# One core, linear attention beside a gated GLU: the last down products of two token groups in seven instead of eight, with their operands formed earlier

## The chip, the cores and the metric

The kernel runs on one core of a Trainium2 chip. The metric is the device time of one execution in microseconds (us), as the median of several runs. Five engines of the core work side by side: TensorE does the matrix products (PE; the load of the operand that stands in the array is shown apart as PEld), VectorE does sums (DVE), ScalarE copies, rounds and evaluates functions (ACT), GpSimd (POOL) and SyncE (SP) issue transfers here. Each engine takes its instructions in the order written.

## The reference

For x of 2048 tokens by 640:

```
g   = sigmoid(sum(x * gate_w))                       # one number a token
q, k, v = x @ wqkv, in 32 heads of 20
phi(t) = where(t > 0, t + 1, exp(t)) + 1e-6
a   = (phi(q) @ (phi(k)^T @ v)) / (phi(q) @ sum(phi(k)) + 1e-6)  @ wo
b   = (sigmoid(x @ w_gate) * (x @ w_up)) @ w_down    # 640 -> 1536 -> 640
out = g * a + (1 - g) * b
```

## The kernel before

**Products.** All operands of the large products are held as a high and a low part in fp32r, and one product of a 128x128 block with 512 tokens is three matmuls: high by high, high by low, low by high (helper `mm3`, lines 406 to 408). The high part of an operand is an ACT copy that rounds (line 419), the low part a DVE subtraction (line 423); the helper `split` does both.

**Fewer products by Strassen's scheme.** Two by two blocks of a product are computed in seven products of sums in place of eight. The names S1 to S4 are sums of blocks of the weight, T1 to T4 sums of blocks of the other operand, A11, B22 and so on are blocks. A partial sum that two results share is computed once, and a result that needs it as its start gets it by an ACT copy from one PSUM bank to another (`seed`); the PE then adds the next product on top of it.

**Stages.** First the k stage (to about 180 us) forms k, v and the weights of the MLP; four chunks of x pass through it, and each chunk's Strassen forms are made in it. Weights whose forms are used twice go to DRAM as formed parts and come back later. Then the 2048 tokens are taken in two halves of two groups of 512: groups 2 and 3 (`pr` is 1 in the code) from about 180 to 405 us, groups 0 and 1 (`pr` is 0) from about 405 us to the end. For each half there is a q phase (q, its feature map) and an f phase that goes through 12 blocks f of 128 of the 1536 hidden columns: gate and up products, sigmoid and product give the hidden block hf; after every second block a pair of f blocks goes down (`down_pair`): its contribution to the 5 x 2 output blocks (5 blocks of 128 output columns, 2 token groups) is added to tb in SBUF by DVE.

**The last pair.** In the pairs before the last, four of the five output blocks are computed in seven products for each two by two set (14 products) and the fifth plainly (4 products), 18 in all. For groups 0 and 1 this holds for the last pair too; its S forms are made during their f phase (`queue_last_s`: two loads, four DVE sums, two splits, two stores to DRAM, then two loads). Three of its outputs are not added by DVE but by a POOL transfer that accumulates into tb (`far`). For groups 2 and 3 the last pair is plain: `last_down` issues 2 x 5 x 2 = 20 products, and in its course queues the scaling of tb by 1 - g (omg, `scaled`) and its store to b_dram.

**Order.** The class `Order` keeps a model of the clock of each engine. Work for ACT and DVE is queued with a cost and a key; `order.fill` places queued work where the model sees room beside the products, `order.need` places it at once because what follows wants it, `order.run` places one item of a kind. Transfers are put on the SP or POOL queue at the place where the code issues them, and a transfer that has to wait holds up those behind it on its queue. Tiles come from pools with a fixed number of buffers, so a load waits for the last reader of the tile that it overwrites.

**Names.** hf: hidden operand or a T form; wd: formed down weights, ds: formed S sums; dst, wst_f: raw weights; rot, dd, cc, ch: PSUM banks (two each); cx, c: intermediate sums; xth and xtl: T forms of x (high, low), fac and wst: raw x in the q phase.

## Time and profile before

| | before |
|---|---|
| median of 3 runs | 728.75 us (728.59 to 729.23) |
| the profiled execution | 728.59 us; its span is 726.9 us, and 1.7 us lie around it |
| PE | 722.2 us busy, 99% of the span, 3563 matmuls |
| DVE | 573.0 us, 79%, 1006 instructions |
| ACT | 364.0 us, 50%, 675 |
| POOL | 101.2 us, 14%, 166 |
| DMA | 176.95 MB, mean 243 GB/s |

How to read the rows: an instruction of the timeline has its start, its duration, engine, line, operation, output<-inputs and shape; what stands in square brackets is the idle time of the engine before it and what ended it. A group of instructions has its count, busy time and mean ns. Matmuls are pipelined: each is shown with 0.39 us, but the next starts 0.227 us after it, and the step from start to start is what counts.

### The profile page before, as it was taken

Reading aid. Unit: us, or ns where it says so; the run is one execution under the profiler, and the core shown is the slowest. Engines: PE = TensorE matmul, PEld = TensorE weight load, DVE = VectorE, ACT = ScalarE, POOL = GpSimd, SP = SyncE. Lnnn points to the kernel's source line nnn. Section 1 sums busy time; section 2 is a strip of 40 time slices with the busy share of each in tenths; the row PEclk is TensorE's granted clock in tenths of the full one; section 3 lists DMA queues with packets and bytes.
Section 4 is the critical chain, followed back from the end, with each engine's and each line's share of the span. In section 5 each row is a group of like instructions: output and inputs, shape, how many; then the busy total and the mean of one; then the engine's idle time right before and its main releaser. Section 6 shows DMA issues by size and latency. Waiting matters only on the chain.

```text
span 726.9 us, 10146 instructions
## 1 busy us (share of the span) xinstructions
PE 722.2 (99%) x3563; PEld 620.8 (85%) x3563; DVE 573.0 (79%) x1006; ACT 364.0 (50%) x675; POOL 101.2 (14%) x166
## 2 busy tenths in 40 slices
PE   9999999999999999999999999999999999999997
PEld 8999999988888888888888888888888888888886
DVE  6889778987687889898989973447585968698895
ACT  6884649357656653535355363454333232354451
POOL 0211101113212211211210031001000001212000
PEclk9999999999999999999999999999999999999999
DMA  8665658698787866567687289879799695979612
GB/s 258 160 181 111 184 130 252 151 338 295 268 313 259 332 223 232 194 223 253 255 322 273 94 295 331 312 233 311 238 329 358 213 363 169 309 280 291 245 59 102
DMA packets 74137, 176.95 MB, mean 243 GB/s; under 512 B 11834, under 2 KB 35402, under 8 KB 70502
## 3 DMA queue, kind: packets, MB, share of 16 engines
q1 hardware_dynamic: 56102, 111.56, 47.7%
q0 software_dynamic: 17840, 64.57, 25.3%
q8 instruction: 28, 0.46, 0.3%
q14 instruction: 23, 0.19, 0.1%
q10 hardware_dynamic: 144, 0.16, 0.1%
HBM read 105.53 MB, written 64.97 MB: 235 GB/s over the span
## 4 chain that ended last, share of the span: by engine, by line
PE 99%; DVE 0%; issue 0%
PE ch L406 11%; PE ch L407 11%; PE ch L408 11%; PE cc L406 9%; PE cc L407 9%; PE cc L408 9%; PE dd L406 7%; PE dd L408 7%; PE dd L407 7%; PE rot L406 6%; PE rot L407 6%; PE rot L408 6%; PE rot L1505 1%; PE rot L494 0%; PE ch L2576 0%; PE cc L2576 0%
## 5 line engine op out<-in xcount | busy, mean ns | idle before, releaser
L419 ACT ACTIVATE c<-ch 128x512 f32<-128x512 f32 x52 | 31.1, 598 | 90.6 <-PE ch L408 90.5
L423 DVE TENSOR_TENSOR hf<-c,hf 128x512 fp32r<-128x512 f32 x78 | 53.1, 687 | 21.5 <-ACT hf L419 21.2
L419 ACT ACTIVATE hf<-c 128x512 fp32r<-128x512 f32 x78 | 47.7, 625 | 26.0 <-DVE c L423 26.0
L423 DVE TENSOR_TENSOR c<-cc,c 128x512 f32<-128x512 f32 x40 | 27.6, 689 | 34.5 <-PE cc L408 22.3
L406 PE MATMUL ch<-xth,ws 128*128 128x512 f32 x112 | 43.7, 390 | 0.0
L408 PE MATMUL ch<-xth,ws 128*128 128x512 f32 x112 | 43.6, 389 | 0.0
L407 PE MATMUL ch<-xtl,ws 128*128 128x512 f32 x112 | 43.6, 389 | 0.0
L423 DVE TENSOR_TENSOR tb<-rot,tb 128x512 f32<-128x512 f32 (+1 forms) x61 | 39.1, 675 | 3.0 <-PE rot L408 3.0
L423 DVE TENSOR_TENSOR c<-c,c 128x512 f32<-128x512 f32 x50 | 34.4, 688 | 3.3 <-ACT c L419 2.7
L406 PE MATMUL dd<-xrh,wg 128*128 128x512 f32 x90 | 35.2, 391 | 0.0
L408 PE MATMUL dd<-xrh,wg 128*128 128x512 f32 x90 | 35.0, 389 | 0.0
L407 PE MATMUL dd<-xrl,wg 128*128 128x512 f32 x90 | 35.0, 389 | 0.0
L419 ACT ACTIVATE c<-dd 128x512 f32<-128x512 f32 x22 | 13.2, 598 | 41.1 <-PE dd L408 41.1
L423 DVE TENSOR_TENSOR tb<-dd,tb 128x512 f32<-128x512 f32 x40 | 27.4, 686 | 7.7 <-PE dd L408 7.6
L406 PE MATMUL cc<-xbh,ws 128*128 128x512 f32 x84 | 32.7, 389 | 0.0
L408 PE MATMUL cc<-xbh,ws 128*128 128x512 f32 x84 | 32.7, 389 | 0.0
L407 PE MATMUL cc<-xbl,ws 128*128 128x512 f32 x84 | 32.7, 389 | 0.0
L419 ACT ACTIVATE dd<-ch 128x512 f32<-128x512 f32 x22 | 12.8, 582 | 33.6 <-PE ch L408 33.6
L423 DVE TENSOR_TENSOR wst<-wst 128x256 f32<-128x256 f32 (+2 forms) x69 | 27.4, 413 | 1.4
L408 PEld LDWEIGHTS ch<-xth,ws 128*128 128x128 f32 x112 | 21.0, 188 | 4.7
L407 PEld LDWEIGHTS ch<-xtl,ws 128*128 128x128 f32 x112 | 21.0, 188 | 4.2
L406 PEld LDWEIGHTS ch<-xth,ws 128*128 128x128 f32 x112 | 21.0, 188 | 4.1
(663 smaller groups left out, 2362.1 us busy)
## 6 DMA issues: line engine op xcount, KB each, us to landing
wf<-ws POOLq DMA_DIRECT2D x12, 1152.0 KB, 7.6
ws<-wf SPq DMA_DIRECT2D x11, 1152.0 KB, 8.6
wst<-wst_f SPq DMA_DIRECT2D x12, 640.0 KB, 5.1
wf<-wg POOLq DMA_DIRECT2D x12, 640.0 KB, 6.9
wd<-wd POOLq DMA_DIRECT2D x12, 640.0 KB, 8.0
wg<-wf SPq DMA_DIRECT2D x12, 640.0 KB, 5.7
wf<-wd SPq DMA_DIRECT2D x10, 640.0 KB, 9.2
xnst<-xn SPq DMA_DIRECT2D x16, 320.0 KB, 4.2
```

The lines of the kernel that those rows point to most:

```text
L406: nc.tensor.matmul(out, l_hi, r_hi, start=first, stop=False, skip_group_check=True)
L407: nc.tensor.matmul(out, l_hi, r_lo, start=False, stop=False, skip_group_check=True)
L408: nc.tensor.matmul(out, l_lo, r_hi, start=False, stop=last, skip_group_check=True)
L419: nc.scalar.activation(out, src, fn, **kw)
L423: nc.vector.tensor_tensor(out, a, b, op=op)
L1505: nc.tensor.matmul(ps[:w, :w], v[:, m, :w], gt[:, m, c0:c0 + w], start=(m == 0), stop=(m == KC - 1))
```

## The change

Four parts:

1. **The last pair of groups 2 and 3** is computed in 18 products like that of groups 0 and 1 (`last_pair` for both, `last_down` and `tail_f` are gone). The order of its products is its own: W, X0, X1, V, Y0, Y1, W, Z0, Z1, W, X0, X1, Z0, Z1, R0, R1, U0, U1, where V is seeded from W, Y from X, R from X, U from R. V, Y0 and Y1 go out by `far`.
2. **Its S forms** are made in the k stage (`queue_ls`), once for both halves: two loads, four DVE sums and four splits of 256 columns, four POOL stores. `queue_last_s` is gone from the f phase of groups 0 and 1. For groups 2 and 3 `load_last_s` loads them (two of 512 KB) on SP, where the last reader of the tile ds allows it.
3. **The T forms of x's second chunk**, which the q phase of groups 0 and 1 needs, are stored to DRAM in the k stage (`store_t`, eight stores on SP) and loaded again (`load_t`, eight loads on SP behind the S forms), in place of four sums and four splits of 512 columns.
4. **What moves with it**: the scaling of tb is queued in the q phase (`queue_scaled`, step 7), its factor is loaded on the POOL queue instead of SP's; the stores of the last two formed wd tiles come behind the pair (`last_stores`); the steps that turn the attention's denominators into a factor (`queue_dens`) are taken at once when they are ready, instead of in their chain's turn, and the loads of that factor come ahead of down weights (wf) on SP.

The heart of the diff:

```diff
+        def store_t(self, *ts):
+            for t in ts:
+                for i, f in enumerate(self.f.t_part(t, self.cs)):
+                    sp.dma_start(xt_dram[:, t, i], f32(f))
...
+    def queue_ls():
+        p, w = FC // 2 - 1, 4 * P
+        wd_dram[p] = dram.tile([P, 2, WF], F32, name=f"wd{p}")
+        raw = qs.tile([P, 2, D], F32, name="qraw", tag="qraw")[:, :, :w]
+        for j in range(2):
+            sp.dma_start(raw[:, j], wst_f[2 * p + j, :, 2, :w])
...
+            split(t[:, 0], t[:, 1], raw[:, j, 2 * q * P:2 * (q + 1) * P])
+            order.then(lambda: gp.dma_start(wd_dram[p][:, :, 2 * D + cs.start:2 * D + cs.stop], f32(t)))
...
-            if c > 1 and n in (2, 5,):
+            for _ in range(({1: 1, 2: 1, 3: 1, 5: 1}, {3: 2, 4: 1, 5: 1})[c - 2].get(n, 0) if c > 1 else 0):
                 order.run("qw")
...
-            pass
+            chunks[1].store_t(1, 0)
...
+                chunks[1].store_t(2, 3)
                 chunks[2].queue()
...
+            if c == 2 and u == 9:
+                queue_ls()
...
-                          lambda g=g, n=n: st["at", g, KC + n](), chain=True)
+                          lambda g=g, n=n: st.get(("at", g, KC + n), lambda: 1e9)(), **{"first" if n else "chain": True})
...
+    def load_last_s(pr=1):
+        p = FC // 2 - 1
+        if pr:
+            t = down_pool[1].tile([P, 2, 8 * P], F32R, name="ds", tag="ds")
+            DS[p] = [t[:, c] for c in range(2)]
+        else:
+            DS[p] = [x2_tile("ds", F32R).rearrange("p a b -> p (a b)") for _ in range(2)]
+        for c in range(2):
+            sp.dma_start(f32(DS[p][c]), wd_dram[p][:, c, 2 * D:])
...
-    def queue_last_s():
...
+    def load_t(t):
+        c = other[1]
+        for i, f in enumerate(c.f.t_part(t, c.cs)):
+            sp.dma_start(f32(f), xt_dram[:, t, i])
...
         if p == FC // 2 - 1:
+            tags = ("cc", "ch") if pr else ("ch", "ch")
             new("W", "dd", "w0", "B11")
-            new("X0", "ch", "A11", "B11")
+            new("X0", tags[0], "A11", "B11")
             seed("V", "dd", "W")
+            yield
             new("X1", "ch", "A11", "B11", 1)
             seed("Y0", "rot", "X0")
             seed("Y1", "rot", "X1")
             yield
...
+            for q in range(2):
+                go(f"X{q}", "S2", "T2", q=q)
+                if pr:
+                    seed(f"R{q}", "rot", f"X{q}")
+                out(f"X{q}", 2 * q, 1)
...
+            for q in range(2):
+                x = f"R{q}" if pr else f"X{q}"
+                go(x, "S3", "T3", q=q)
+                seed(f"U{q}", tags[q] if pr else "rot", x)
+                out(x, 2 * q + 1, 1)
...
             go("U0", "A22", "T4")
             out("U0", 1, 0)
             go("U1", "A22", "T4", q=1)
             out("U1", 3, 0)
...
-    def last_down(pr, units):
...
-        for i in units:
-            g, o = divmod(i, KC)
-            down_unit(pr, FC - 2, o, g, early.pop(i, None))
...
+    def queue_scaled():
...
+            gp.dma_start(omg[:, g], gate_dram[1, (2 + g) * TG:(3 + g) * TG].partition_broadcast(P))
```

**PE, last pair of groups 2 and 3.** Before, the products of the plain pair alternate over four PSUM banks (dd and rot):

```order
L406 MATMUL rot_4098<-hf,wd 128x512
L407 MATMUL rot_4098<-hf,wd 128x512
L408 MATMUL rot_4098<-hf,wd 128x512
L406 MATMUL dd_4102<-hf,wd 128x512
L407 MATMUL dd_4102<-hf,wd 128x512
L408 MATMUL dd_4102<-hf,wd 128x512
L406 MATMUL rot_4106<-hf,wd 128x512 [waits DVE_49]
```

Now the same place holds the seeded products: X1, V (dd_4125) and Y0 (rot_4133), of which the last two wait for an ACT copy:

```order
L407 MATMUL ch_4129<-hf,wd 128x512
L408 MATMUL ch_4129<-hf,wd 128x512
L409 MATMUL ch_4129<-hf,wd 128x512
L407 MATMUL dd_4125<-hf,wd 128x512 [waits Activation_49]
L408 MATMUL dd_4125<-hf,wd 128x512 [waits DVE_49]
L409 MATMUL dd_4125<-hf,wd 128x512
L407 MATMUL rot_4133<-hf,wd 128x512 [waits Activation_49]
```

And at the end of the pair R0 (rot_4195), R1 (rot_4201) and U0 (cc_4215) follow one another:

```order
L407 MATMUL rot_4195<-hf,ds 128x512 [waits Activation_49]
L408 MATMUL rot_4195<-hf,ds 128x512 [waits DVE_49]
L409 MATMUL rot_4195<-hf,ds 128x512
L407 MATMUL rot_4201<-hf,ds 128x512 [waits Activation_49]
L408 MATMUL rot_4201<-hf,ds 128x512
L409 MATMUL rot_4201<-hf,ds 128x512
L407 MATMUL cc_4215<-hf,wd 128x512 [waits Activation_49]
```

What moved: PE now takes results that it has itself just finished, by way of a copy on ACT, for seven of the 18 products.

**ACT, the same pair.** Before, the sigmoid of the last hidden block (cx<-cx) is the second instruction in the stretch of the pair, and forms for the next phase follow:

```order
L419 ACTIVATE hf<-c_3877 128x512
L419 ACTIVATE cx<-cx 128x512
L419 ACTIVATE hf<-cx 128x512
L419 ACTIVATE xrh<-wst 128x256
L419 ACTIVATE wg<-dst 128x640
```

Now the seeds of V (dd), Y0 and Y1 (rot) stand around that sigmoid, the one of V ahead of it, those of Y behind it:

```order
L420 ACTIVATE hf<-c_3910 128x512
L420 ACTIVATE xah<-wst 128x2x256
L420 ACTIVATE dd_4125<-dd_4117 128x512
L420 ACTIVATE cx<-cx 128x512
L420 ACTIVATE rot_4133<-cc_4121 128x512
L420 ACTIVATE rot_4135<-ch_4129 128x512
L420 ACTIVATE hf<-cx 128x512
L420 ACTIVATE hf<-c_3798 128x512
```

What moved: the copies of which PE has need share ACT's order with the sigmoid, which itself waits for DVE.

**SP, from the last raw weights to the q phase.** Before, the raw weights of q follow those of the last f blocks:

```order
L363 DMA dst<-wst_f 128x640 x2
L363 DMA dst<-wst_q 128x640
L363 DMA wu<-wq_1857 128x768
L363 DMA ws<-wq_1985 128x2304
L363 DMA ds<-gate_dram 128x512 x2
L363 DMA wg<-wq_1854 128x1280
```

Now the S forms and the T forms stand between them, and the factor from gate_dram is gone from this queue:

```order
L364 DMA dst<-wst_f 128x640 x2
L364 DMA ds<-wd_1295 128x1024 x2
L364 DMA xth<-xt_dram 128x2x256
L364 DMA xtl<-xt_dram 128x2x256
L364 DMA xth<-xt_dram 128x2x256
L364 DMA xtl<-xt_dram 128x2x256
L364 DMA xth<-xt_dram 128x2x256
L364 DMA xtl<-xt_dram 128x2x256
L364 DMA xth<-xt_dram 128x2x256
L364 DMA xtl<-xt_dram 128x2x256
L364 DMA dst<-wst_q 128x640
L364 DMA wu<-wq_1890 128x768
```

What moved: ten loads now stand ahead of the weights of the q phase.

More of the change, by code (lines that the diff above doesn't have):

```diff
@@ L1560, in rest @@
         def rest():
-            if j == 0:
+            if p not in wd_dram:
                 wd_dram[p] = dram.tile([P, 2, WF], F32, name=f"wd{p}")
             gp.dma_start(wd_dram[p][:, :, (1 - j) * D:(2 - j) * D], f32(t))
-            if p == FC // 2 - 1:
-                load_d()
-        order.then(rest)
+        if p == FC // 2 - 1:
+            last_stores.append(rest)
+        else:
+            order.then(rest)
     def queue_ds(p):
@@ L1906, in far @@
         def far(key, o, g):
-            if not far_at:
+            if not far_at and order_pr[0]:
+                t = f32(wd_tile())
+                far_at.extend((t[:, 0], t[:, 1], down_pool[1].tile([P, D], F32, name="far", tag="dst", bufs=2)))
+            elif not far_at:
                 far_at.extend(down_pool[1].tile([P, D], F32, name="far", tag=n) for n in ("mr", "mv"))
@@ L1934, in down_pair, with zs @@
             yield
[L1935 to L1938 removed]
+            def zs():
+                new("Z0", "ch" if pr else "cc", "S1", "T1")
+                out("Z0", 1, 1)
+                new("Z1", "cc", "S1", "T1", 1)
+                out("Z1", 3, 1)
+            if not pr:
+                zs()
             go("V", "w1", "B21")
@@ L1966, in down_pair @@
             return
-        if pr:
-            for j in range(2):
-                order.need(("d", ("f", 1, 2 * p + j)))
         new("W", "dd", "w0", "B11")
@@ L2254, in scaled @@
             gp.dma_start(b_dram[:, o, g], tb[:, o, g])
-        for i in units[:4]:
-            g, o = divmod(i, KC)
-            early[i] = ps_tile("rot" if (o + g) % 2 else "dd")
-            down_term(early[i], pr, FC - 2, o, g, True)
-        for i in units:
-            g, o = divmod(i, KC)
-            down_unit(pr, FC - 2, o, g, early.pop(i, None))
+        for i in range(2 * KC):
             order.add(0, v_cost(TG), lambda i=i: scaled(i), ("tb", i),
-                      lambda: order.vec + 0.6, lazy=True)
-            order.fill()
-        order.slack(False)
+                      lambda: max(order.vec + 0.6, order.when(omg)), lazy=True)
     order.need((nx[1], 2))
```

209 lines of the change are left out of this document (95 added, 114 removed).

## The prediction

> **What bounds the kernel now.** I read the page first, then the waits, the timeline of PE at the place of the change, then ACT, DVE and SP there.
>
> ```profile
> PE 722.2 (99%) x3563; PEld 620.8 (85%) x3563; DVE 573.0 (79%) x1006; ACT 364.0 (50%) x675; POOL 101.2 (14%) x166
> PE 99%; DVE 0%; issue 0%
> PE rot L494 <- PEq L2765: 0.8, 1, 0.8
> ```
>
> PE is busy in 99% of the span, the chain that ended last is PE alone, and the one wait of PE lies at the start. So the time is the number of matmuls times their step, and nothing else counts unless it makes PE wait. Work taken from DVE, ACT or a queue is worth nothing here; work added to them costs only where a product then comes late. The profiled execution took 728.59 us, 0.16 under the median of 728.75; the sum below is a difference, and I put it on the median.
>
> The last pair of groups 2 and 3 on PE, first and last product of 20 (60 matmuls), with the last matmul ahead that reads ds, and the first of the q phase:
>
> ```profile
> 389.76 0.39 PE L408 MATMUL cc<-hf,ds 128*128 128x512 f32 x1
> ...
> 392.03 0.39 PE L406 MATMUL dd<-hf,wd 128*128 128x512 f32 x1
> ...
> 405.40 0.39 PE L408 MATMUL rot<-hf,wd 128*128 128x512 f32 x1
> 405.63 0.39 PE L406 MATMUL ch<-xah,wg 128*128 128x512 f32 x1
> ```
>
> From 392.03 to 405.63 are 13.60 us for 60 matmuls: a step of 0.2267 us with no gap, 0.68 us a product.
>
> **The gain.** 18 products in place of 20 are 6 matmuls fewer: 6 x 0.2267 = -1.36 us (0.19%). Nothing else takes matmuls away, so this is also the most that can be won. The Trainium skill, page "TensorE: Matmul & The Clock Gate", section "Back-to-back issue gap", gives 512/2.4 + 2.5, some 216 ns, for an isolated stream of this width; the six would then be worth -1.29 us, an estimate from that page. The rows differ and go first.
>
> **What the new order makes PE wait for.** Plain products start from weights and hidden operands alone. Seven of the new ones start from an ACT copy of a result just finished. The price of such a handover shows at the end of groups 0 and 1, where the same scheme runs already: X0's last matmul, X1, W (dd), then U0, which starts from a copy of X0.
>
> ```profile
> 654.50 0.39 PE L408 MATMUL ch<-hf,ds 128*128 128x512 f32 x1
> ...
> 655.41 0.39 PE L406 MATMUL dd<-hf,wg 128*128 128x512 f32 x1
> ...
> 656.09 0.39 PE L406 MATMUL rot<-hf,wg 128*128 128x512 f32 x1
> 654.99 1.26 ACT L419 ACTIVATE rot<-ch 128x512 f32<-128x512 f32 x2 [2.50 <-PE ch L408]
> L419 ACT ACTIVATE dd<-ch 128x512 f32<-128x512 f32 x22 | 12.8, 582 | 33.6 <-PE ch L408 33.6
> ```
>
> ACT starts 0.49 us after the start of the last matmul that it waits for, and a copy takes 0.58. What follows until PE runs is seen where PE was released by ACT at the last moment:
>
> ```profile
> 178.77 0.60 ACT L419 ACTIVATE c<-ch 128x512 f32<-128x512 f32 x1 [0.19 <-PE ch L408]
> 179.46 0.46 PE L406 MATMUL ch<-xth,wu 128*128 128x512 f32 x1
> 179.75 0.40 PE L407 MATMUL ch<-xtl,wu 128*128 128x512 f32 x1
> ```
>
> The copy ends at 179.37; the matmul stands at 179.46, but the next follows 0.29 after it in place of 0.23, so it ran some 0.06 late: 0.15 from copy to product. A handover is 0.49 + 0.58 + 0.15 = 1.22 us, against 0.2267 for each matmul that stands between.
>
> *U0.* Between R0's last matmul and U0 stands only R1: 4 steps, 0.91 us, where groups 0 and 1 have W as well, 7 steps, 1.59 us and no wait. PE waits 1.22 - 0.91 = 0.31. U1 comes after its own 4 steps plus that 0.31: 0.
>
> *Y0.* X1 and V lie between X0 and Y0 (7 steps), but ACT is not free:
>
> ```profile
> 393.03 0.69 DVE L423 TENSOR_TENSOR cx<-cc,cx 128x512 f32<-128x512 f32 x1
> 393.76 0.63 ACT L419 ACTIVATE cx<-cx 128x512 f32<-128x512 f32 x1 [3.72 <-DVE cx L423]
> 398.76 0.62 ACT L419 ACTIVATE b12h<-wst 128x512 fp32r<-128x512 f32 x1
> 407.25 0.60 ACT L419 ACTIVATE c<-ch 128x512 f32<-128x512 f32 x1 [7.87 <-PE ch L408]
> ```
>
> (b12h there is the last work of ACT before an idle of 7.87 us, so later seeds find it free.) The sigmoid waits for DVE until 393.72, and the seed of Y0 stands behind it. Sigmoids and copies follow each other some 0.1 before the end shown, so the seed runs 394.28 to 394.86 and Y0 can start at 395.01. It is due 12 matmuls after 392.03, at 394.75: a wait of 0.26. Behind it everything on PE moves; the seed of Y1 ends by 395.42 and Y1 is due at 395.69: 0.
>
> *V, Z, R.* V's copy starts at 392.48 + 0.49 = 392.97 and is done at 393.55, V due at 394.07. X0 needs DVE's last read of its bank, tb<-cc:
>
> ```profile
> 391.83 0.69 DVE L423 TENSOR_TENSOR tb<-cc,tb 128x512 f32<-128x512 f32 x1
> 395.87 0.69 DVE L423 TENSOR_TENSOR hf<-cx,hf 128x512 fp32r<-128x512 f32 x1 [0.76 <-ACT hf L419]
> ```
>
> It ends at 392.52 and X0 is due at 392.71: 0, by 0.19. The hidden operand that is formed last (low part done at 396.56; now its high part stands behind both seeds on ACT, so about 396.7) is wanted by the tenth product, 27 matmuls after 392.03 plus 0.26, at 398.4. R0 has 10 steps or more after X0's second product: 0. DVE has fewer additions than before, since three outputs go out by an ACT copy and a POOL accumulate. The accumulates wait for ACT and for DVE's earlier addition; behind them on POOL stand the two stores of formed wd tiles, which are read again only in the f phase of groups 0 and 1, and the q phase's stores.
>
> Sum of the pair: -1.36 + 0.31 + 0.26 = -0.79 us. Bounds of the waits: none at all (if the 0.15 is not paid and DVE is a little earlier), or twice 0.57.
>
> **The load of the S forms.** The two ds loads of 512 KB go out when the last matmul on the old ds ends, 389.76 + 0.39, about 390.2, and Z0, 21 matmuls after 392.03 plus 0.26, wants the first at 397.05, the second at 397.5. Behind them on SP wait eight loads of 256 KB and then the weights of the q phase.
>
> ```profile
> 388.00:391.00 3.00, 3.00 (x15) 2.50 (x14) 3.00 (x6) 2.04 (x4) 0.12 (x1) 1.00 0.00 0
> 394.00:397.00 3.00, 3.00 (x15) 2.47 (x14) 2.14 (x4) 2.18 (x5) 0.00 (x0) 1.00 1.03 411
> 630.86 1.13 SPq L363 DMA_DIRECT2D ds<-wd  x2
> ds<-wd SPq DMA_DIRECT2D x2, 512.0 KB, 7.6
> DMA to landing us min/median/max: 4.6/7.4/10.1
> 390.62 0.33 SPq L363 DMA_DIRECT2D dst<-wst_q  x1
> 396.05 0.72 ACT L419 ACTIVATE wg<-dst 128x640 fp32r<-128x640 f32 x1
> ```
>
> (The first two rows are windows: busy times of PE, PEld, DVE, ACT and POOL, granted clock, DMA share and GB/s; the fifth is of the tile ds.) At 388 to 391 the DMA engines are idle, and 3 us later they move 411 GB/s. Early bound: issue to 391.3 as at 630.86, then 1 MB at 411 GB/s, 2.6 us: 394. Late bound: 10.1 us after the second issue at 391, 401, a wait of 3.6. In between, the median of 7.6, from a stretch with full queues: 398.6, a wait of 1.1. I take 394 to 396, as the row with 0 GB/s is of this very place, and 0. What stands behind is later too: dst<-wst_q went out at 390.62 and was formed from 396.05 on; behind 3 MB at 411 GB/s it lands near 400. Its first reader on PE comes 104 matmuls after 392.03, at 415: covered by 10 us or more.
>
> On this the Trainium skill, page "DMA: Bandwidth & Descriptors", section "Issuing engines are not separate DMA queues", speaks against the change: all transfers run on the same 16 engines and interleave. Its section "Bandwidth" has 6.15 us for 1 MB, by which the loads would land at about 397, an estimate, just in time. Whether the xt loads push in between is the third rival.
>
> **The rest, which I cost at 0 or a risk.** *k stage:* added are 8 + 2 transfers on SP, 4 on POOL, and 4 sums and 4 splits of 256 columns, by the row below 8 x 0.41 = 3.3 us of DVE; moved are qw forms.
>
> ```profile
> L423 DVE TENSOR_TENSOR wst<-wst 128x256 f32<-128x256 f32 (+2 forms) x69 | 27.4, 413 | 1.4
> 60.00:76.00 16.00, 16.00 (x110) 16.00 (x109) 12.00 (x23) 7.47 (x17) 1.19 (x1) 1.00 0.57 138
> 116.00:145.00 29.00, 29.00 (x192) 28.38 (x192) 27.11 (x51) 15.38 (x27) 3.57 (x3) 1.00 0.81 213
> ```
>
> At 60 to 76 DVE has 4 us free in 16 and DMA stands at 0.57, which hides it. At 116 to 145 DVE has 1.9 free in 29: one form late there would stall PE by up to its own 0.7. *q phase:* removed are, among others, these (of 405 to 421):
>
> ```profile
> L423 DVE TENSOR_TENSOR wst<-wst 128x512 f32<-128x512 f32 x4 | 2.8, 688 | 0.1
> L423 DVE TENSOR_TENSOR xtl<-wst,xth 128x512 fp32r<-128x512 f32 x4 | 2.7, 684 | 0.0
> L406 PEld LDWEIGHTS ch<-xth,ws x6: 187/188/188, 419.1 to 424.5; 128*128 128x128 f32 x6
> ```
>
> PE has no wait there to win back. The T forms are first read at 419, some 20 us after they land; the omg load now stands behind stores on POOL, and the scaled tb is read only at the end. *Groups 0 and 1:* the seven-product pair stays; the earlier factor steps put loads ahead of wf on SP, some 2 us for the worst of them:
>
> ```profile
> 610.65 2.49 SPq L363 DMA_DIRECT2D fac<-fac_dram  x4
> 614.29 1.88 SPq L363 DMA_DIRECT2D wf<-wd  x3
> 627.50 0.40 PE L406 MATMUL dd<-hf,wf 128*128 128x512 f32 x1
> ```
>
> wf has 13 us from issue to use there; 512 KB of stores beside it are gone. 0 taken, up to 1 us late.
>
> **Forecast (0.45).** 728.75 - 0.79 = 727.96, 728.0 us, -0.11%; its own range 727.5 to 728.6. A measurement of this kernel can tell about 0.2%, 1.46 us, from no change, so this is "the same".
>
> **Rivals.** *No wait at all (0.17):* -1.36, 727.4. For it: the seeds of groups 0 and 1 cost none; against it: the one R1 between R0 and U0. *Small waits elsewhere (0.15):* DVE at 116 to 145 or wf late, 0.7 to 1.9 us: 728.7 to 729.9, the gain given back. *The S forms late (0.2), slower:* the xt loads or queue latency delay ds. Landing at 398.3 eats the gain; each us after it is a us. From 399.8 on the kernel is slower by over 0.2%; at the late bound, 401.1: 727.96 + 3.6 = 731.6. For it: if all ten loads share the engines evenly, 3 MB at 411 GB/s take 7.7 us, from 391 to 398.7, a wait of 1.2 and 729.2, and a little latency on top does the rest. Against it: an empty queue and their being first in it. The Trainium skill, same page, section "Two DMAs through the same engine are not ordered", says that descriptors of one queue start in order, and all ten loads stand on SP's; no run here has shown it yet. *The relief counts (0.03):* PE has no wait to free, below 727.3 only by scatter.
>
> Faster by over 0.2%, at 727.29 or less: 0.13, the lower edge of the no-wait case with scatter of the runs and the relief. Slower, above 730.21: 0.2, the late S forms beyond 399.8 (0.14) and several small waits together (0.06). The same: 0.67. Range for 8 in 10: 727.2 to 730.7.
>
> **What would show it.** After: 3557 PE matmuls; a gap of some 0.26 ahead of the first rot<-hf,wd of the pair and 0.31 ahead of the second last product's cc<-hf,wd; no gap at ch<-hf,ds; the pair about 12.8 us long; no gap in 116 to 145, nor at 627. A gap at ch<-hf,ds, or a wait of PE on a DMA, makes it wrong.

## The result

The changed kernel takes 731.3 us (median of 7 runs, 731.0 to 732.27), the kernel before 729.23 in the runs beside it (7, 728.59 to 730.8): a ratio of 1.0030, 95% interval 1.0018 to 1.0041. It is slower by 0.3%. The profiled execution took 731.15 us; its span is 729.4.

From the page of the kernel after: the engines' busy time, the chain that ended last by engine, and then all the waits of PE over 0.2 us (total, times, longest, in us):

```profile
PE 723.2 (99%) x3557; PEld 619.2 (85%) x3557; DVE 573.3 (79%) x1008; ACT 369.7 (51%) x686; POOL 106.5 (15%) x173
PE 89%; DMA 5%; DVE 3%; ACT 2%; issue 1%; SPq 0%
PE dd L407 <- DVE gt L424: 1.3, 1, 1.3
PE rot L495 <- PEq L2789: 0.8, 1, 0.8
PE rot L407 <- DVE tb L424: 0.2, 1, 0.2
```

Six matmuls fewer are there (3557), and yet the chain is no longer PE alone: 11% of it runs through DMA, DVE, ACT and issue. The busy figure hides what happened, since PE reads as 99% busy before and after. What counts is where it falls behind. If each matmul after is set against the same matmul before, in the two profiled executions, PE is late by:

| place | late behind it, us | added there |
|---|---|---|
| the first 6 us | 0.14 | +0.14 |
| k stage, 136 us | 0.48 | +0.34 |
| k stage, 144 us | 2.07 | +1.59 |
| to the last pair of groups 2 and 3 (small steps) | 2.19 | +0.13 |
| the last pair | 1.56 | -0.63 |
| q phase, 417 us | 1.91 | +0.35 |
| groups 0 and 1, 627 us | 2.25 | +0.34 |
| groups 0 and 1, 639 us | 2.84 | +0.59 |

The last product ends at 725.92 us and not at 723.08. The pair gives 0.63 us of its 1.36; four places that the change only touches take 3.2 us.

**The k stage.** The rows of the timeline after, of DVE, POOL, SP, ACT, DVE and PE (start, duration; in brackets the idle time before and what ended it):

```profile
117.10 0.76 DVE L424 TENSOR_TENSOR qp<-qraw,qp 128x256 fp32r<-128x256 f32 x2
119.12 1.19 POOL L364 DMA_DIRECT2D zacc<-kb  x1 [3.82 <-DVE logit L848]
119.87 1.95 POOL L364 DMA_DIRECT2D wd<-qp  x2
125.08 0.98 SPq L364 DMA_DIRECT2D xz<-xt  x2
130.32 0.85 ACT L420 ACTIVATE xrh<-xz 128x768 fp32r<-128x768 f32 x1 [4.29 <-DMA xz<-xt]
133.42 0.85 ACT L420 ACTIVATE xbh<-xz 128x768 fp32r<-128x768 f32 x1 [2.26 <-DMA xz<-xt]
134.30 0.96 DVE L424 TENSOR_TENSOR xbl<-xz,xbh 128x768 fp32r<-128x768 f32 x1 [1.74 <-ACT xbh L420]
143.63 0.88 DVE L424 TENSOR_TENSOR gt<-dd,gt 128x320 f32<-128x320 f32 x2
142.58 0.39 PE L409 MATMUL ch<-xah,wg 128*128 128x512 f32 x1
144.27 0.47 PE L407 MATMUL dd<-xrh,wg 128*128 128x512 f32 x1 [1.30 <-DVE gt L424]
```

and the same load, DVE and PE before:

```profile
114.04 2.11 SPq L363 DMA_DIRECT2D xz<-xt  x2
131.31 0.96 DVE L423 TENSOR_TENSOR xbl<-xz,xbh 128x768 fp32r<-128x768 f32 x1
140.65 0.88 DVE L423 TENSOR_TENSOR gt<-dd,gt 128x320 f32<-128x320 f32 x2
142.33 0.39 PE L406 MATMUL dd<-xrh,wg 128*128 128x512 f32 x1
```

The load of x for groups 2 and 3 goes out 11 us later than before. Its tile xz lies in memory that the pool of raw weights (qs) gives back, and that pool now also holds the S forms (qp) until their stores have been read out. DVE ends the last two splits of the S forms at 117.86, 3.8 us after this load went out before. Their stores then stand on POOL behind an accumulate (zacc<-kb) and land at 124.97; xz goes out at 125.08, and in the runs below too it goes out 0.01 to 0.12 us behind the last of these landings. ACT then idles 4.3 and 2.3 us for it, DVE is 3.0 us later with xbl, stays 3.0 us later down to gt<-dd, and PE stands 1.46 us for the bank that gt frees. Of these 3.0 us, 0.88 are there ahead of the first form of xz (xal<-xst starts at 126.19 and not at 125.31), about as much as the two splits at 117.10 and the start; nearly all the rest is idle time for xz.

**The pair.** First the start (dd), then X0, Y0, U0 and the first product of the q phase on PE, and the copies on ACT that the last two wait for:

```profile
394.22 0.39 PE L407 MATMUL dd<-hf,wd 128*128 128x512 f32 x1
394.90 0.47 PE L407 MATMUL cc<-hf,wd 128*128 128x512 f32 x1
395.21 0.39 PE L408 MATMUL cc<-hf,wd 128*128 128x512 f32 x1
396.82 0.39 PE L409 MATMUL dd<-hf,wd 128*128 128x512 f32 x1
397.22 0.50 PE L407 MATMUL rot<-hf,wd 128*128 128x512 f32 x1
397.56 0.39 PE L408 MATMUL rot<-hf,wd 128*128 128x512 f32 x1
405.31 0.39 PE L409 MATMUL rot<-hf,ds 128*128 128x512 f32 x1
405.69 0.50 PE L407 MATMUL cc<-hf,wd 128*128 128x512 f32 x1
407.19 0.40 PE L407 MATMUL ch<-xah,wg 128*128 128x512 f32 x1
396.59 0.58 ACT L420 ACTIVATE rot<-cc 128x512 f32<-128x512 f32 x1
405.05 0.58 ACT L420 ACTIVATE cc<-rot 128x512 f32<-128x512 f32 x1 [1.40 <-PE rot L409]
DMA to landing us min/median/max: 4.8/4.8/4.8
```

It is 12.97 us long (394.22 to 407.19) in place of 13.60. Y0 stands 0.40 us behind the matmul ahead, 0.18 more than a step, and the next one 0.34 behind it, 0.11 more again: 0.29. U0 costs 0.38 - 0.23 + 0.11 = 0.26 in the same way, X0 0.08. The 0.10 that is left of 12.97 - 54 x 0.2267 = 0.73 is spread over steps of 0.23 to 0.24 behind them. The last row is of the tile ds: issued at 392.4 and 392.75, the S forms land within 4.8 us, at 397.5, and no product waits for them.

**Groups 0 and 1.** Here wf are down weights, M's rows (mt<-m_dram) are rows of the matrix that the sums over k and v make with wo, and p (pl<-p_dram) is the feature map of q, which DVE scales by the factor. POOL, SP and DVE after, the transfer of wf, and PE at the two places:

```profile
615.37 4.60 POOL L364 DMA_DIRECT2D mt<-m_dram  x8
615.57 2.33 SPq L364 DMA_DIRECT2D wf<-wd  x3
wf<-wd SPq DMA_DIRECT2D x2, 640.0 KB, 12.0
632.98 0.69 DVE L428 SCALAR_TENSOR_TENSOR pl<-pl,fac 128x512 f32<-128x512 f32 x1 [3.49 <-DMA pl<-p_dram]
627.17 0.39 PE L409 MATMUL ch<-xth,ws 128*128 128x512 f32 x1
627.60 0.50 PE L407 MATMUL dd<-hf,wf 128*128 128x512 f32 x1
639.72 0.50 PE L407 MATMUL rot<-hf,wf 128*128 128x512 f32 x1 [0.22 <-DVE tb L424]
```

and before:

```profile
617.50 4.59 POOL L363 DMA_DIRECT2D mt<-m_dram  x8 [4.01 <-DMA wd<-mt]
632.41 0.68 DVE L427 SCALAR_TENSOR_TENSOR pl<-pl,fac 128x512 f32<-128x512 f32 x1
625.47 0.39 PE L406 MATMUL dd<-hf,wf 128*128 128x512 f32 x1
```

Before, POOL stood 4 us at the store of the S form (wd<-mt) ahead of the eight loads of M's rows, which so started 3.2 us behind wf. That store is gone, the rows start 0.2 us ahead of wf, and the first load of wf takes 12.0 us. Before, it took at most 11.2, since PE read it at 625.47 without a wait (the landing on record there is that of the second load, 11.1). The load of p takes as long as before (15.0 and 15.4 us) but goes out 1.7 us later, lands at 632.95, and DVE idles 3.5 us in front of its scaling, with the additions that free PE's banks queued behind it; before, the scaling stood further back in DVE's order and p was there.

### The profile page after: what moved, and what is told of

Read it like the earlier page. It is cut to its first block, busy times and chain, and to the rows that moved or that the text cites. A ratio compares the mean times of both kernels' runs of the same rounds, so it can differ in the third digit from the quotient of the medians.

```text
span 729.4 us, 10205 instructions
## 1 busy us (share of the span) xinstructions
PE 723.2 (99%) x3557; PEld 619.2 (85%) x3557; DVE 573.3 (79%) x1008; ACT 369.7 (51%) x686; POOL 106.5 (15%) x173
## 4 chain that ended last, share of the span: by engine, by line
PE 89%; DMA 5%; DVE 3%; ACT 2%; issue 1%; SPq 0%
PE ch L407 10%; PE ch L409 10%; PE ch L408 10%; PE cc L407 8%; PE cc L409 8%; PE cc L408 8%; PE dd L407 7%; PE dd L409 7%; PE dd L408 7%; PE rot L407 5%; PE rot L409 5%; PE rot L408 5%; DMA pl<-p_dram 2%; DMA xz<-xt 1%; DMA wg<-wq 1%; DMA wg<-wd 1%
## 5 line engine op out<-in xcount | busy, mean ns | idle before, releaser
L424 DVE TENSOR_TENSOR tb<-rot,tb 128x512 f32<-128x512 f32 (+1 forms) x58 | 37.3, 676 | 3.0 <-PE rot L409 3.0
L424 DVE TENSOR_TENSOR tb<-dd,tb 128x512 f32<-128x512 f32 x36 | 24.7, 687 | 6.6 <-PE dd L409 6.5
L424 DVE TENSOR_TENSOR wst<-wst 128x256 f32<-128x256 f32 (+1 forms) x65 | 24.7, 396 | 1.4
L424 DVE TENSOR_TENSOR tb<-cc,tb 128x512 f32<-128x512 f32 x36 | 24.6, 687 | 1.2 <-PE cc L409 1.2
L409 PEld LDWEIGHTS ch<-xth,ws 128*128 128x128 f32 x112 | 21.0, 188 | 4.7 <-DVE ws L424 0.3
```

Source lines behind the costliest of these rows:

```text
L409: nc.tensor.matmul(out, l_lo, r_hi, start=False, stop=last, skip_group_check=True)
L424: nc.vector.tensor_tensor(out, a, b, op=op)
```

## The experiments

Times are medians, the ratio is to the kernel before in the same session, with its 95% interval. "Late" is worked out as above.

| run | us (runs) | ratio |
|---|---|---|
| the changed kernel | 731.3 (7) | 1.0030 (1.0018 to 1.0041) |
| e1 stores on SP | 731.45 (10) | 1.0030 (1.0018 to 1.0043) |
| e2 factor steps in turn | 732.38 (5) | 1.0037 (1.0024 to 1.0050) |
| e3 T loads last | 733.02 (4) | 1.0052 (1.0035 to 1.0069) |
| e4 pair, both seeds first | 735.19 (4) | 1.0078 (1.0063 to 1.0093) |
| e5 pair, one seed first | 732.5 (4) | 1.0052 (1.0037 to 1.0066) |
| e6 M's rows later | 732.06 (4) | 1.0045 (1.0032 to 1.0058) |
| e7 e1, e5 and e6 together | 731.3 (6) | 1.0038 (1.0025 to 1.0051) |
| e8 T forms computed | 731.87 (4) | 1.0038 (1.0023 to 1.0052) |
| e9 scaling later | 731.7 (4) | 1.0035 (1.0021 to 1.0048) |
| e10 four edits | 729.95 (11) | 1.0014 (1.0005 to 1.0023) |
| e11 M's rows on SP | 730.88 (10) | 1.0022 (1.0013 to 1.0031) |
| e12 five edits | 729.57 (11) | 1.0009 (0.9999 to 1.0019) |
| e13 order behind the late load | 731.7 (5) | 1.0040 (1.0028 to 1.0053) |
| e14 e12, R between | 730.18 (11) | 1.0009 (1.0000 to 1.0018) |
| e15 e14, planner told | 731.39 (12) | 1.0026 (1.0013 to 1.0039) |

### The k stage: e1 and e13

```diff
 # e1
-            order.then(lambda: gp.dma_start(wd_dram[p][:, :, 2 * D + cs.start:2 * D + cs.stop], f32(t)))
+            order.then(lambda: sp.dma_start(wd_dram[p][:, :, 2 * D + cs.start:2 * D + cs.stop], f32(t)))
```

> The four stores of the S forms in the k stage are issued on SP instead of POOL; the work is the same. Theory 1 (memory): in the changed kernel the load of xz waits until 125.1 us for the last of these stores, since xz lies in memory that they read, and they stand behind an accumulate on POOL; DVE then waits for xz and PE for DVE at 144 us. By it xz goes out some 3 us earlier, and the waits of PE at 136.5 to 144.3 (1.8 us together) fall to 0.3 or less: about 729.6 us. Rival (work): DVE is late at 144 because it has 3.3 us more to do in the k stage. By it the wait at 144 stays at 1.0 or more: about 731.2 us.

The waits between 136 and 144 us are gone, though the sums and splits are the same, and at 367 us PE is hardly later than it was at 6 us (0.85 against 0.80; the first 6 us took longer in this execution). So the extra work alone does not make PE wait there. The load:

```profile
124.27 1.03 SPq L364 DMA_DIRECT2D xz<-xt  x2
```

The last store landed at 124.26 and xz went out at 124.27: on either queue the landing of the stores holds the load, so the shared memory is what delays it. POOL's accumulate is little of it: without it the load goes out 0.8 us earlier, where the theory had 3. So the load is late here too, and PE does not wait. DVE's order had changed with the edit: the additions gt now stand ahead of the sums of xz. Little of the 1.9 us won is left at the end. In the profiled execution 0.7 is: it began 0.66 us later than that of the changed kernel, and at 416, 626 and 638 us PE lost 0.47, 0.74 and 0.73 us in place of 0.35, 0.34 and 0.59. The medians show nothing of it: the time is the rival's, though the rival's wait is gone. And in the four kernels below that have this edit beside others (e7, e10, e12, e14) PE does lose 0.3 to 0.6 us near 180 us, in three of them waiting for a copy on ACT (c).

```diff
 # e13: the planner's clock of SP's queue alone, the transfers are the same
-            nx[1].load(((0, 0, 2), (0, 2, KC), (1, 0, KC)))
+            nx[1].load(((0, 0, 2),))
+            sp.t = sp.t + 15
+            nx[1].load(((0, 2, KC), (1, 0, KC)))
```

> The changed kernel, its transfers and their queues as they are; only the planner's clock of SP's queue is put 15 us later ahead of the load xz<-xt, so that DVE's order has the additions gt<-dd, gt<-cc and gt<-rot ahead of the sums and forms of xz. Theory: the load goes out at 125 us again and lands at 130 to 133.4, since nothing frees its memory earlier, and PE's wait of 1.46 us at 144 goes all the same: it is the order of DVE behind a load later than the order assumes. The time falls by 0.5 to 1.8 us, less what later waits take: 729.5 to 730.8 us. Rival: the late load as such is what PE waits for (the forms of xz are wanted soon after); then a wait of 1 us or more shows at the first product that reads them, and the time is 731 us or more.

The load, DVE's gt, and the waits of PE:

```profile
125.34 0.98 SPq L364 DMA_DIRECT2D xz<-xt  x2
140.67 0.88 DVE L424 TENSOR_TENSOR gt<-dd,gt 128x320 f32<-128x320 f32 x2
PE dd L407 <- DVE ms L848: 0.6, 1, 0.6
PE cc L407 <- DVE c L424: 0.5, 1, 0.5
```

With the load as late as in the changed kernel, gt comes at 140.67 as it did before the change, and the wait at 144 is gone. But DVE still has the work that it could not do while xz was missing (it is busy 14.0 us from 130 to 146 us, and 15.9 before the change), and PE now stands at 179.6 (0.74), 183.2 (0.74 with the next step) and 189.2 (0.50): behind 190 us it is 2.0 us later than at 6 us, as in the changed kernel (1.9). The wait at 144 went as the theory said, but the time is the rival's: with a load this late, the order decides where PE pays, not whether. Why e1 paid next to nothing with a load 0.8 us earlier is not settled in full; its second part was used from 131.40 on and not from 133.42, and DVE's order behind it was another.

### The pair: e4 and e5

```diff
 # e4: both seeds of Y ahead of the sigmoid, W x B22 behind what the q phase needs
-        tail[4]()
-        if not pr:
+        if pr:
             next(down)
-        next(down)
+            tail[4]()
+        else:
+            tail[4]()
+            next(down)
+            next(down)
...
-                go("W", "w1", "B22")
-                out("W", 4, 1)
...
+            go("W", "w1", "B22")
+            out("W", 4, 1)
             go("U0", "A22", "T4")
 # e5: one seed ahead of the sigmoid; W x B22 ahead of what the q phase needs
+            go("W", "w1", "B22")
+            out("W", 4, 1)
             if pr:
                 order.need((nx[1], 2))
                 order.need(("wg", ("q", 0, 4)))
-            else:
-                go("W", "w1", "B22")
-                out("W", 4, 1)
```

> In the last pair of groups 2 and 3 the product W (w1 by B22) moves between R1 and U0, and the copies that seed Y0 and Y1 stand ahead of the sigmoid on ACT. Theory: a seeded product waits when fewer than 1.22 us of other products stand between it and its source, or when its copy stands behind the sigmoid. By it the waits at Y0 (0.29 us) and U0 (0.26 us) are gone and the pair, from its first product to the first of the q phase, takes 12.3 to 12.4 us in place of 13.0: about 730.7 us. Rival: the sigmoid that comes 1.1 us later makes the hidden operand late, and its first reader waits 0.3 us or more: no gain.

The waits at Y0 and U0 are gone, but X0's product with T2 waits 0.45 us for the hidden operand whose sigmoid both seeds had delayed. And W's addition, now behind the forms of x and wg on DVE, held the bank dd. PE, and then two windows (busy times of PE, PEld, DVE, ACT and POOL with their counts, granted clock, DMA share, GB/s):

```profile
408.92 0.39 PE L409 MATMUL ch<-xah,wg 128*128 128x512 f32 x1
411.36 0.47 PE L407 MATMUL dd<-xrh,wg 128*128 128x512 f32 x1 [2.06 <-DVE tb L424]
408.00:411.30 3.30, 1.30 (x6) 0.75 (x4) 3.30 (x8) 2.76 (x6) 0.00 (x0) 1.00 1.07 261
411.30:415.00 3.70, 3.64 (x10) 2.92 (x11) 3.70 (x7) 1.23 (x3) 0.00 (x0) 0.59 1.04 366
```

2.2 us of standing, and a granted clock of 0.59 behind it: PE is 3.9 us later by 416 us. The pair itself took 0.40 us less than the plain one, where the changed kernel's takes 0.63 less.

> The product W x B22 moved to stand between the R products and U0, ahead of what the pair waits for, and of Y's two seeds only the first put ahead of the sigmoid. Theory: the waits at Y0 (0.29 us) and U0 (0.26 us) are what is left over in the pair and both go, and since the sigmoid is late by one seed (0.55 us) and not by two (1.1 us, which cost 0.45 us at X0 x T2), nothing takes their place: 731.3 - 0.55 = 730.7 us. Rival: the addition from W's tile, now the last of the pair's, again holds the q phase's product in dd (2.4 us the last time), so over 732 us.

Y0 and U0 again wait for nothing, and X0 x T2 neither: one seed's delay fits, and the pair's products take 1.08 us less than the plain ones. But the q phase's product in dd waited once more, for 0.49 us (0.6 with the next step) and by another cause: the low part xrl of x, which stood on DVE behind the pair's additions. So the pair won nothing, and a wait of 0.48 for wf at 554 us, which no other of these executions has, and the same waits as ever near 639 did the rest. In e12 the additions of R's products come behind the forms that the q phase needs; there the pair, from 392.92 to 405.42, takes 12.50 us, 1.10 less than the plain one.

### The T forms: e3 and e8

```diff
 # e3
-        (FC - 1, 7): [lambda: [load_t(t) for t in (1, 0, 2, 3)], queue_b],
+        (FC - 1, 7): [queue_b],
...
         load_forms("q", 0, 1, 2)
+        for t in (1, 0, 2, 3):
+            load_t(t)
 # e8: the same line without load_t, and
-        for ns, t, k in (((0, 1, 2), 1, 3), ((), 0, 4), ((), 2, 5), ((3,), 3, 6)):
...
+        queue_both(nx)
```

> The eight loads of T forms stand on SP behind the loads of the q weights instead of ahead of them. Theory: the wait at 417.4 (0.32 us, PE on the load wg) comes from the q weights that land late behind 2 MB of T forms; by it that wait is gone and no other comes, since the T forms are first read at 420: about 731.0 us. Rival: wg is late because it goes out when PE leaves its tile, 6.6 us before its use, whatever stands ahead; then the wait stays: about 731.3 us. No wait at ch<-hf,ds in either.

Neither theory nor rival: the wait at 417 grew from 0.32 to 0.90, and that for wf at 628 from 0.32 to 0.72. The T loads were then the ones in flight beside the load that PE waits for there (wg<-wq, issued at 410.5): two of them landed only at 415.7 and 416.4.

> The T forms of x's second chunk computed again on ACT and DVE as in the kernel before, and not loaded; their stores in the k stage are kept, so that everything ahead of 394 us is the same. Theory: the DRAM route is worth little by itself, since DVE and ACT have room in the q phase, and costs the q weights some DMA time: the wait at 417 (0.21 us) goes, nothing else comes, 731.0 to 731.3 us. Rival: the last pair's additions and these eight operations (some 4 x 0.69 us of sums and 4 forms of 0.7 us on DVE, 5.5 us) don't fit together, and PE waits for a form of x behind the pair: over 732 us.

The wait at 417 is gone, and the eight operations more on DVE and ACT cost nothing there. The windows from 405 to 421 us of before, after and e8, in this order:

```profile
405.00:421.00 16.00, 16.00 (x78) 13.49 (x77) 14.44 (x24) 8.98 (x16) 1.02 (x2) 1.00 0.32 106
405.00:421.00 16.00, 15.95 (x75) 12.85 (x74) 15.27 (x26) 12.25 (x23) 0.56 (x1) 1.00 0.92 309
405.00:421.00 16.00, 16.00 (x77) 12.99 (x75) 15.90 (x28) 12.34 (x23) 1.25 (x3) 1.00 0.57 189
```

The change raises the share of the DMA engines there from 0.32 to 0.92, and without the T loads it is 0.57. The landings on record of the T loads lie ahead of this window (the last at 403.9); what they do is push back the transfers behind them (ws<-wq lands at 411.8 and not, as in e8, at 402.7). The load wg goes out at 410.8 in both. The 0.32 won at 417 were waited away at 627 (0.71 in place of 0.32) and 639 (1.0 in place of 0.6), so nothing is left of it in the time.

### Groups 0 and 1: e2, e6, e9 and e11

```diff
 # e2
-                          lambda g=g, n=n: st.get(("at", g, KC + n), lambda: 1e9)(), **{"first" if n else "chain": True})
+                          lambda g=g, n=n: st["at", g, KC + n](), chain=True)
 # e6
-        (FC - 1, 4): [lambda: load_ms(0), a_first],
+        (FC - 1, 4): [a_first],
         (FC - 1, 5): [a_fifth],
+        (FC - 1, 6): [lambda: load_ms(0)],
 # e9
-            ... lambda u=u: order.when(t[u]) + 1, lazy=True)
+            ... lambda u=u: order.when(t[u]) + 4, lazy=True)
 # e11
-            m_rows(raw[j].rearrange("p (k c) -> p k c", c=P), slice(c0, c0 + P), gp)
+            m_rows(raw[j].rearrange("p (k c) -> p k c", c=P), slice(c0, c0 + P), (sp, gp)[i])
```

> The factor steps of the denominators are again taken in their chain's turn, as in the kernel before; all else is the changed kernel. Theory: the loads of the factor ahead of wf make wf late at 627.6 (0.32 us of waits) and the load of pl late, behind which DVE's additions stand, so that PE waits at 639.7 (0.49 us). By it both waits are gone: about 730.5 us, and the wait at 144 stays as it is. Rival: the later PE time alone (2 us) shifts these transfers against each other; then the waits stay: about 731.3.

The wait at 627 went, those near 639 stayed and became three of 0.26 to 0.40 us (each with 0.11 at the next matmul): DVE still idled 3.4 us for p. In that execution the second load of wf took 14.3 us and PE came 0.7 us later than in the changed kernel, so that the factor steps alone are not shown to be the cause.

> The eight loads of M's rows in groups 0, 1 issued two steps later (at step 6 of the last block and not at step 4). Theory: in the kernel before, the stores of the S form (wd<-mt) stood on POOL's queue ahead of these loads, which started at 617.5 us; without them they start at 615.4, together with the load wf<-wd that PE waits for at 627.17, and both share the DMA engines. With them later, wf lands at least 0.3 us earlier and the wait of 0.32 us at 627.2 goes, p lands earlier too and the wait of 0.49 us at 639 at least halves: 730.5 to 730.8 us. Rival: the wf load is late only because its tile is freed when it is; then wf lands at 627.4 to 627.7 again, both waits stay, and the time is 731.3.

Nothing was won, because the edit did not do what it was for. Seven of the eight loads on POOL's queue:

```profile
615.88 4.02 POOL L364 DMA_DIRECT2D mt<-m_dram  x7
```

POOL has nothing ahead of these loads that lasts, so an issue written two steps later goes out 0.5 us later. This says nothing about the theory.

> The planner holds the scaling pl<-pl,fac on DVE until 4 us, and not 1 us, behind the modelled landing of p, so that in DVE's order it stands behind tb<-dd, c, hf, hf, tb<-dd and tb<-ch as in the kernel before, and not ahead of them. Theory: the waits of PE near 639 us come from this place alone (DVE idle 3.5 us with PE's additions queued behind): both go, DVE has no idle time over 1 us between 629 and 634, and PE is 0.5 to 0.6 us less late behind 640: 730.7 us. The wait at 627, on wf's own load, stays. Rival: DVE is late there because everything on it is; then waits of the same sum come at tb<-rot or at the scaling's new place, 731.3.

The theory holds for 639: no wait is left there, and DVE, which had idled 3.5 us, reaches the first addition at 631.64 in place of 633.58. The time did not follow, since in the profiled execution the waits at 417 and 627 came to 0.72 and 0.50 and the start was 0.6 us later.

> The changed kernel with the eight loads of M's rows issued on SP's queue behind wf, p and ws, and not on POOL's, where nothing holds them back any more (writing them two steps later moved them by 0.5 us only). Theory: in the kernel before, POOL stood 4.0 us at the store of the S form until 616.90, and M's rows started at 617.50, 3.2 us behind wf's load; now they start with it or before it and make it last 12 to 13.8 us instead of 11.1. On SP they come after it: wf takes 11 us or less, lands by 626.8, and the wait of 0.32 us at 627.2 goes; p lands 1 us earlier, so that the waits near 639 halve: 730.5 to 730.9 us. Rival: the DMA engines are full with SP's own loads from 614 us on; wf takes 12 us again and the wait stays: 731.3.

The transfers of wf and p, and DVE's scaling:

```profile
wf<-wd SPq DMA_DIRECT2D x2, 640.0 KB, 8.1
pl<-p_dram SPq DMA_DIRECT2D x2, 256.0 KB, 11.0
630.55 0.69 DVE L428 SCALAR_TENSOR_TENSOR pl<-pl,fac 128x512 f32<-128x512 f32 x1
```

wf lands in 8.1 us and not in 12.0, p in 11.0 and not in 15.0, and both waits are gone, those near 639 as well, with DVE's order as in the changed kernel. On SP the rows go out at 632.3 only, when wf and p have landed. So 640 KB of M's rows in eight small loads, in flight beside them, are what held wf and p. This agrees with the Trainium skill, page "DMA: Bandwidth & Descriptors", section "Issuing engines are not separate DMA queues": a second queue saves issue time only, the transfers share the engines. It is the one edit that alone has a lower ratio than the changed kernel (1.0022 and 1.0030), but the intervals overlap. In its profiled execution PE came to 627 us 1.1 us later than in the changed kernel, which is less than the 3.6 us by which the first load of wf was ahead of its use.

### Together: e7, e10, e12, e14, e15

e7 is e1, e5 and e6 in one kernel.

> The changed kernel with the stores of the S forms on SP's queue, W x B22 and the first seed as in the run before, and M's rows later. If the three causes add, the changed kernel's own gain of 1.36 us is left with little to set against it: 731.3 - 1.8 (k stage) - 0.55 (pair) - 0.5 to 0.8 (groups 0, 1) = 728.2 to 728.5 us, 0.5 to 0.8 under the kernel before. If the stages behind are held by DMA that does not start earlier, part of each gain is waited away at 417, 627 and 639: 729.5 to 730.5.

It came out at the changed kernel's 731.3, above both forecasts. The pair was as in the single run, the k stage lost 0.5 us near 180 us that e1 had not lost, and PE was 0.5 us late at 616; then it waited 1.0 us at 626 and 0.9 at 638. What is won ahead of a stage that is held by transfers is waited away in it.

e10 is e1, e2 and e9 with the pair of e5, W's addition ahead of those of R.

> The changed kernel with the stores of the S forms on SP's queue (k stage), W x B22 between R1 and U0 with its addition ahead of R's and Y0's seed ahead of the sigmoid (pair), the factor steps in the chain's turn (wait at 627) and the scaling later on DVE (wait at 639). Theory: each wait has its own cause, so all go but the one at 416 (0.1 to 0.5 us): PE ends 0.9 to 1.4 us ahead of the kernel before apart from the first 6 us, 727.6 to 728.4 us. Rival: groups 0, 1 wait for DMA that is busy from 614 us on and starts no earlier when PE does; then 1 us or more of the gain is waited away between 625 and 640, and the time is 728.7 to 729.5.

The time lies past the rival's as well, and only part of the loss is the rival's: 0.47 at 627, where wf, issued from 614.1 on as in the kernel before, took 13.8 us (its second load) beside M's rows from 613.9 on. The rest is 0.62 near 180 us, 0.41 at 417, and 0.62 with the next step for dd, which was held for xrl again.

e12 adds e11 to it, puts R's additions behind the forms of x and wg, and the scaling at 5 us.

> The run with four edits again, with M's rows on SP's queue as in the run beside this, and R's additions behind the forms that the q phase waits for on DVE. Theory: of the waits left in that run (0.62 us at 406.9 for xrl behind additions, 0.47 at 416, 0.47 at 626, some 0.5 between 160 and 180) the first and the third go: 729.95 - 0.62 - 0.47 = 728.9 us, level with the kernel before. Rival: the forms come earlier but the R tiles are freed later and the q phase waits for them at 412, and wf's load is as long without M's rows: 729.9 again.

Its page and the only wait of PE over 0.2 us:

```profile
PE 722.4 (99%) x3557; PEld 620.2 (85%) x3557; DVE 573.0 (79%) x1008; ACT 369.1 (51%) x686; POOL 99.2 (14%) x161
PE 99%; DVE 0%; issue 0%
PE rot L495 <- PEq L2793: 0.9, 1, 0.9
```

The chain is PE alone again, and the second load of wf took 9.4 us. The waits for xrl and at 626 went, as the theory said; the time lies between theory and rival. Counted from 6 us on, PE ends 0.29 us earlier than in the kernel before: 1.10 are won in the pair, 0.25 lost up to 240 us, 0.14 to 391, 0.32 at 412 and 416 and 0.1 at 494. The runs give 1.0009 (0.9999 to 1.0019): level with the kernel before, not better.

```diff
 # e14, against e12
                 order.need((nx[1], 2))
+                out("R0", 1, 1)
+                out("R1", 3, 1)
                 order.need(("wg", ("q", 0, 4)))
-                out("R0", 1, 1)
-                out("R1", 3, 1)
```

> The run with five edits, with R's additions on DVE between the forms of x and those of wg, and not behind both. Theory: the waits of 0.19 us near 412 go and nothing else changes: 729.4 us, by the profile 0.2 under the run with five edits. Rival: no change at all, 729.6.

The same ratio as e12, and the waits near 412 stayed: the rival.

e15 is e14 with the stores on POOL and the edit of e13 in place of e1.

> As the run beside this, but with the stores of the S forms on POOL's queue as in the changed kernel and the planner told of the late load instead. Theory: both ways serve, so that the time is that of the run beside this within 0.3 us, about 729.4. If the order behind the late load costs less than eight more issues on SP's queue, it is 0.2 to 0.5 us less: 728.9 to 729.2, level with the kernel before.

Neither: it is slower, at 731.39. Here PE lost 0.74, 0.75 and 2.1 us at 180, 184 and 191 us, the longest for a copy on ACT, and 3.7 us in all up to 200 us, where e14 lost 0.6. The ratios of the two, 1.0026 and 1.0009, have intervals that hardly overlap. Telling the planner does not replace having the load earlier.

## Why the prediction was wrong, step by step

*The gain* of 1.36 us is there: 3557 matmuls, and the pair was at best 12.50 us long (e12) where 54 steps alone would be 12.24.

*U0 and Y0:* 0.26 and 0.29 measured against 0.31 and 0.26. The handover from the rows of groups 0 and 1 (0.49 + 0.58 + 0.15 = 1.22) holds as a sum: for U0 it was 0.42 + 0.58 + 0.17 = 1.17. *X0* was said to be due 0.19 us behind DVE's last read and cost 0.08. The sum of the pair was -0.63 against -0.79: 0.08 of the difference is X0, 0.10 the small steps.

*The load of the S forms:* right in its result, no gap at ch<-hf,ds. It landed at 397.5 and not at 394 to 396, having gone out 2.2 us later than the step assumed, because PE was that late by then. The rival that all ten loads would share the engines and delay it did not come: the T loads behind it landed from 399.5 to 403.9. The Trainium skill, page "DMA: Bandwidth & Descriptors", section "Two DMAs through the same engine are not ordered", has the descriptors within one queue of one engine start in order; the landings of this execution agree.

*The step that failed* is the k stage at 0. It counted DVE's work (3.3 us) and set it against DVE's free time, and named 0.7 us as the most that one late form would cost. It also looked for room at 60 to 76 us, but the S forms were made from 106 to 117.9. The extra work alone was not the loss (e1). The S forms kept a pool's memory until their stores had landed, and the load of x that takes over this memory went out 11 us later. The waits of ACT, DVE and PE follow from that load in the timeline and cost 1.93 us with the small ones ahead of it. How much of it is owed to the load alone stays open, since e1 with a load 0.8 us earlier paid nothing in its profiled execution, and e15 with one 0.4 us later paid 3.7. The step listed what is added and moved on each queue, but not who gets the memory next.

*Groups 0 and 1* were put at "0 taken, up to 1 us late", with the 512 KB of stores that are gone counted on the good side. They were 0.93 us late. The step gave wf 13 us from issue to use, by the row at 627.50, but that is the tenth matmul that reads it: the first stands at 625.47, 11.2 us from issue, so there was next to no room. And the missing store counted on the bad side: it had held M's rows back behind wf (with the rows out of the way both waits go, e11 and e12). For the 0.59 at 639 us the place of the scaling in DVE's order is enough as a cause too (e9). *The q phase at 0* missed 0.35: dst and the weights were covered as said, but not the load of wg at 410.8, which went out when PE left its tile and met DMA engines at 92%; in e8, issued at the same time with the engines at 57%, it made no wait.

So the forecast's pair was right to 0.16 us, and of the rivals it was the small waits elsewhere that came, with "DVE at 116 to 145" and "wf late" both named, but at 0.35 to 1.93 us each and all at once (3.2 us) where the rival had 0.7 to 1.9 in all. The signs that it named for the pair and the S forms were there; the gaps at 144 and 627 us and the waits for a DMA at 417 and 627 are those by which it called itself wrong.

## What to carry to other kernels

When work with tiles of its own is moved into an earlier stage, look up which tile takes over that memory and what its load waits for, down to the landing of the last store; the planner of this kernel did not see it. A store that makes a queue wait can be what keeps the transfers behind it out of the way, so what is taken off a queue has to be checked for what then starts earlier. And a gain on the engine that bounds a kernel lasts only to the next stage whose transfers do not start earlier with it: the chain of waits must be free to the end, as in the run with five edits.

## What the runs showed that was not expected

- When PE had stood for a bank or a load, the step behind it was longer too, 0.335 us in place of 0.227 in most cases and 0.306 at 144 us, so a wait costs 0.08 to 0.11 us more than its gap. The prediction had 0.06 for it.
- After 2.2 us of standing (e4) the granted clock fell: seven matmuls of 512 columns followed each other at 0.427 us. After 1.5 us (the changed kernel, 144 us) and 1.97 us (e15, 191 us) it did not. The Trainium skill, page "TensorE: Matmul & The Clock Gate", Part 1, has a half clock after an idle window of some 3.4 us that runs free of the program, the full clock after some 3.4 us of work, and 426.7 ns for such a step. The step and the length of the slow stretch (411.9 to 415.2) agree, but the standing was shorter than the window here.
- The first 6 us differ by up to 0.8 us between the profiled executions (0.80 in e1, 0.14 in the changed kernel, -0.05 in e7). So in the comparison of two single executions these first 6 us stand apart, as in the table of the late places.
